# Transposing the gate weights before the output projection's backward pass, and adding the gate biases as one-row matmuls

## The chip, the cores and the metric

The kernel runs on one core of one Trainium2 chip. The metric is device time in microseconds (us); lower is better. Most executions agree within 0.3%. Quoted times are medians. A profile is one execution; its span is some 1.8 us shorter than the measured time (763.3 us against 765.1 us for the profiled execution of the kernel before). Engines: PE (matmul), DVE (VectorE), ACT (ScalarE), POOL (GpSimd), SP (SyncE, which here only issues transfers).

## The reference, cut to what matters

One decode step of a gated attention block, with its backward pass. Outputs are the result and the gradients of nine inputs.

```python
xn = _layernorm(x)
s  = A(xn)    # 32 query heads, 8 KV heads, attention over the last 4096 of 32768 cached rows, then @ wo
g  = silu(B(xn))              # relu(xn @ w1 + b1)**2 @ w2 + b2 : the "gate"
return x + s * g
# reference(): out, and vjp(grad_out) with respect to x, k_cache, v_cache, wq, wo, w1, b1, w2, b2
```

The gradients of the two caches have the caches' full shape, 2 x 8 x 32768 x 128 in bf16. Only the last 4096 rows of each head get a gradient; the other 28672 must be written as zeros. That is 2 x 16 x 28672 x 128 x 2 B = 235 MB of zeros, in 32 parts of 7.34 MB.

## The kernel before

GpSimd queues 31 of the 32 parts of zeros ("zero fills"), from a zeroed tile. They wait only for the load of `wo`, never for arithmetic:

```python
for qi in range(ZQ - 1):                      # ZQ = 32
    ...
        r = zf(*zparts[qi], r, n, rows, rep)  # nc.gpsimd.dma_start(out=v, in_=zeros)
```

The start, cut to the parts that the change touches. Weights and the first V load go into one SP queue; the biases are loaded spread over 128 partitions:

```python
b1_bf = pw.tile([P, FK], BF16, name="b1_bf")       # 128 pieces of 28 B
dma_store.dma_start(out=b1_bf[:], in_=B_b1.rearrange("(p j) -> p j", j=FK))
b2_bf = pw.tile([P, DK], BF16, name="b2_bf")       # 128 pieces of 8 B
dma_store.dma_start(out=b2_bf[:], in_=B_b2.rearrange("(p k) -> p k", k=DK))
dma_load.dma_start(out=w1, ...); dma_load.dma_start(out=w2, ...)   # both in one buffer, tag "k"
wo_in = dma_load.dma_start(out=wo[:], ...); dma_load.dma_start(out=wq[:], ...)
vnat = load(A_v_cache, 0, "v")
... # transposes of x and grad_out; casts b1T<-b1_bf, b2T<-b2_bf; layernorm
... # hps = w1.T @ xn (56 matmuls); hBT = hps + b1T; relu, square; ups = w2.T @ h (56); uT = ups + b2T; silu
... # do_rows, doT_all: backward pass of the output projection (transposes of wo, matmuls)
... # q_rows, qT_all: query projection
for g0 in range(0, len(jobs), 8):                  # 112 transposes of w1 and w2 -> w1T, w2T
    ...
knat = load(A_k_cache, 0, "k")                     # takes over the buffer of w1 and w2
for r in range(NR):                                # 4 rounds of 4 KV heads
    ... # scores of V (dp), scores of K (s), softmax, p_bf, ds_bf
    outer_store(p_bf, bddo, vnat, out_3, r)        # overwrites vnat, stores it
    if r + 1 < NR: vnat = load(A_v_cache, r + 1, "v")
    ...
    outer_store(ds_bf, bdq, knat, out_2, r)
    if r + 1 < NR: knat = load(A_k_cache, r + 1, "k")
```

So the first K load waits for the last gate-weight transpose, and every later load waits for a store. The end:

```python
... # weight gradients; dw2 store; last, in 16 pieces:
        evac(dw1_st[:, k, n0:n0 + n], wps[:, 0:n])
last = nc.sync.dma_start(out=out_6.rearrange("(p k) f -> p k f", k=DK), in_=dw1_st)   # last weight store, 1.8 MB
with tc.issue_after(last.ins):
    fin = nc.sync.dma_start(out=v, in_=zs)                                            # final fill, 7.34 MB
tc.add_manual_dep(fin.ins, sw_fill[-2].ins.name, ...)     # waits for the last-but-one GpSimd fill
```

## Time and profile before

| | before |
|---|---|
| time, median of 3 | 765.2 us (765.09 to 765.24) |
| bytes moved by DMA | 326.73 MB at 428 GB/s |
| end of arithmetic = issue of the last weight store | 724.6 us |
| first K load issued / landed | 95.5 / 123.0 us |

These are lines of the page of the kernel before. The "busy tenths" give the busy share in 40 equal slices of the span, 9 being 90% or more; the queue lines give packets, megabytes and the share of the 16 DMA engines' time:

```profile
PE 387.6 (51%) x4118; PEld 233.5 (31%) x4118; DVE 275.8 (36%) x483; ACT 214.6 (28%) x313; POOL 34.0 (4%) x67
...
DMA  9999999999999999999999999999999999999998
GB/s 382 443 416 422 451 412 425 444 435 416 430 432 450 416 439 429 426 427 446 414 431 435 437 428 427 429 433 440 425 436 437 432 434 422 428 441 425 422 428 379
DMA packets 11833, 326.73 MB, mean 428 GB/s; under 512 B 2898, under 2 KB 2906, under 8 KB 2934
...
q0 software_dynamic: 7360, 227.55, 70.5%
```

The DMA row has no hole: 39 slices of 40 are at 9, and 428 GB/s hold from start to end, while PE is busy 51% of the span. Queue q0 carries the fills, 70% of the bytes. The Trainium skill, "DMA: Bandwidth & Descriptors", section "Specifications", gives 435 GB/s as the ceiling of the fabric; the trace, at 98% of it, agrees.

The windows view shows busy time per engine (with numbers of instructions), the granted PE clock, the DMA share and GB/s in chosen stretches, here near the end of the kernel before:

```profile
core 0: us, PE busy (x) PEld busy (x) DVE busy (x) ACT busy (x) POOL busy (x), PEclk, DMA share, GB/s
...
700.00:720.00 20.00, 18.72 (x43) 5.53 (x42) 13.77 (x22) 12.27 (x21) 0.00 (x0) 0.50 1.04 429
720.00:740.00 20.00, 3.76 (x10) 1.03 (x8) 3.06 (x6) 2.95 (x6) 0.00 (x0) 0.50 0.98 421
740.00:760.00 20.00, 0.00 (x0) 0.00 (x0) 0.00 (x0) 0.00 (x0) 0.00 (x0) 0.50 0.99 424
```

Arithmetic is over soon after 720 us, yet DMA runs at 421 to 424 GB/s until 760 us. These are queued stores and the final fill.

In the timeline of the start, the columns are start, duration, engine, line, operation, tiles; in brackets, how long the engine had been idle and what ended it:

```profile
20.52 0.17 DVE L248 CAST b2T<-b_bf 128x4 f32<-128x4 bf16 x1 [8.93 <-DMA b_bf<-in_B_b_dram]
20.60 0.16 DVE L244 CAST goT<-tp 128x8 f32<-128x8 bf16 x1
...
20.82 1.86 PE L158 MATMUL pp<-xT_f,ones_f 128*128 128x2 f32 x8 [12.72 <-DVE goT L244]
```

On DVE the cast of b2 stands ahead of that of grad_out (`goT`). DVE waits 8.9 us for the landing of b2 (8-byte pieces, issued at 2.0 us), and only after that casts grad_out, whereupon PE starts the layernorm sums, having idled 12.7 us. The transfers that SP issues, in the same columns ("SPq" is SP's queue):

```profile
95.46 0.53 SPq L210 DMA_DIRECT2D nat<-in_A_k_cache_dram  x1
...
507.46 0.54 SPq L210 DMA_DIRECT2D nat<-in_A_k_cache_dram  x1
...
724.57 0.33 SPq L639 DMA_DIRECT2D out_dram<-dw  x1
725.00 0.42 SPq L644 DMA_DIRECT2D out_dram<-zt  x1
```

The chain of waits (start, duration, what) puts long stretches down to K loads. Two of its entries:

```profile
95.46 27.58 DMA nat<-in_A_k_cache_dram
...
507.46 48.59 DMA nat<-in_A_k_cache_dram
```

This chain led back from the last arithmetic. Whether its length is also what the time depends on is the question of this case.

### The profile page before, as it was taken

To read this page: it belongs to the slowest core of one execution; us is meant where nothing else is said; L and a number is where in the kernel's file an instruction comes from. 1 tells how busy PE (TensorE), PEld (TensorE's weight loads), DVE (VectorE), ACT (ScalarE), POOL (GpSimd) and SP (SyncE) were. 2 spreads that over 40 slices of the span, in tenths; PEclk is the share of its full clock that TensorE was granted. 3 is DMA by queue.
4 is the path that set the end of the run, shared out by engine and by line. 5 is a ranking of instruction groups with operands and counts; after the bars stand their busy time and mean duration, and the time that the engine had idled before them with its cause. 6 is when DMAs were issued, how large, how long until landed. Compare 5 with 4: busy or idle time off the path is not lost.

```text
span 763.3 us, 9400 instructions
## 1 busy us (share of the span) xinstructions
PE 387.6 (51%) x4118; PEld 233.5 (31%) x4118; DVE 275.8 (36%) x483; ACT 214.6 (28%) x313; POOL 34.0 (4%) x67
## 2 busy tenths in 40 slices
PE   0666774477003648850576673015073775866800
PEld 0533553333002435420244430014053343423200
DVE  3333342485002347540344653003045152666600
ACT  0144521455000244540112553002013231722500
POOL 0200100010000000000000000000000000000000
PEclk9987997778556886775578587559585675855555
DMA  9999999999999999999999999999999999999998
GB/s 382 443 416 422 451 412 425 444 435 416 430 432 450 416 439 429 426 427 446 414 431 435 437 428 427 429 433 440 425 436 437 432 434 422 428 441 425 422 428 379
DMA packets 11833, 326.73 MB, mean 428 GB/s; under 512 B 2898, under 2 KB 2906, under 8 KB 2934
## 3 DMA queue, kind: packets, MB, share of 16 engines
q0 software_dynamic: 7360, 227.55, 70.5%
q1 hardware_dynamic: 2696, 56.63, 20.9%
q10 hardware_dynamic: 1736, 41.95, 13.2%
q8 instruction: 32, 0.52, 0.3%
q14 instruction: 9, 0.07, 0.0%
HBM read 45.62 MB, written 280.50 MB: 427 GB/s over the span
## 4 chain that ended last, share of the span: by engine, by line
DMA 36%; PE 31%; DVE 12%; ACT 9%; issue 6%; ACTq 0%; DVEq 0%; SPq 0%
DMA nat<-in_A_k_cache_dram 18%; DMA out_dram<-nat 15%; PE ov L421 7%; PE tp L387 4%; ACT nat L150 3%; ACT p_bf L455 2%; DMA b_bf<-in_B_b_dram 2%; PE ps L410 2%; DVE nat L152 2%; ACT tring L150 2%; DVE ds_bf L468 2%; PE s_ps L394 2%; PE wps L588 2%; PE dops L314 2%; PE tp L310 1%
## 5 line engine op out<-in xcount | busy, mean ns | idle before, releaser
L387 PE MATMUL tp<-pperm,nat 128*128 128x128 bf16 x1024 | 91.8, 242 | 180.0 <-DMA nat<-in_A_v_cache_dram 130.0
L152 DVE COPY tring<-tp 128x1024 bf16<-128x1024 bf16 (+1 forms) x98 | 66.1, 689 | 211.0 <-PE tp L387 201.8
L387 PEld LDWEIGHTS <-nat 128*128 128x128 bf16 x1024 | 68.4, 109 | 200.1 <-DMA nat<-in_A_v_cache_dram 131.9
L150 ACT COPY tring<-tp 128x1024 bf16<-128x1024 bf16 (+1 forms) x34 | 34.4, 1011 | 260.2 <-PE tp L387 235.5
L150 ACT CAST nat<-ov 128x512 bf16<-128x512 f32 x160 | 87.4, 590 | 63.6 <-PE ov L421 62.8
L152 DVE CAST nat<-ov 128x512 bf16<-128x512 f32 x96 | 65.5, 690 | 54.3 <-PE ov L421 51.8
L101 POOL DMA_DIRECT2D out_dram<-zt x58 | 32.5, 565 | 529.1 <-DMA out_dram<-zt 507.8
L421 PE MATMUL ov<-bd,ds_bf 128*128 128x512 bf16 x128 | 48.6, 455 | 5.7 <-DVE nat L152 3.7
L421 PE MATMUL ov<-bd,p_bf 128*128 128x512 bf16 x128 | 48.7, 452 | 4.2 <-DVE nat L152 1.4
L410 PE MATMUL ps<-t,nat 128*128 128x16 bf16 x1024 | 28.7, 173 | 14.5 <-issue 7.6
L410 PEld LDWEIGHTS <-nat 128*128 128x128 bf16 x1024 | 28.7, 102 | 17.3 <-issue 12.2
L394 PEld LDWEIGHTS <-zz 128*32 128x32 bf16 x512 | 17.4, 94 | 34.0 <-issue 24.0
L152 DVE CAST wq<-wps 128x512 bf16<-128x512 f32 x16 | 11.0, 690 | 44.2 <-PE wps L581 44.0
L394 PE MATMUL s_ps<-tring,zz 128*32 128x256 bf16 x256 | 19.9, 299 | 12.0 <-ACT tring L150 6.9
L402 PE MATMUL tp<-ident_bf,p_bf 128*128 128x128 bf16 x64 | 7.5, 312 | 34.9 <-ACT p_bf L455 34.9
L150 ACT CAST wq<-wps 128x512 bf16<-128x512 f32 x16 | 9.4, 585 | 53.3 <-PE wps L581 53.3
L455 ACT ACTIVATE p_bf<-e_sb,rl 32x512 bf16<-32x512 f32 x16 | 22.8, 1424 | 3.4 <-DVE rl L452 3.3
L394 PE MATMUL dp_ps<-tring,zz 128*32 128x256 bf16 x256 | 19.4, 305 | 7.7 <-ACT tring L150 4.6
L468 DVE SCALAR_TENSOR_TENSOR ds_bf<-dp_ps,delta,p_bf 32x512 bf16<-32x512 f32 x16 | 21.7, 1359 | 0.2
L421 PEld LDWEIGHTS <-ds_bf 128*128 128x128 bf16 x128 | 12.9, 107 | 20.4 <-issue 17.9
L421 PEld LDWEIGHTS <-p_bf 128*128 128x128 bf16 x128 | 12.8, 109 | 19.8 <-issue 17.1
L402 PEld LDWEIGHTS <-p_bf 128*128 128x128 bf16 x64 | 6.5, 146 | 36.0 <-ACT p_bf L455 36.0
(195 smaller groups left out, 444.4 us busy)
## 6 DMA issues: line engine op xcount, KB each, us to landing
out_dram<-zt POOLq DMA_DIRECT2D x23, 7168.0 KB, 96.7
out_dram<-nat ACTq DMA_DIRECT2D x8, 4096.0 KB, 40.9
out_dram<-zt POOLq DMA_DIRECT2D x7, 3584.0 KB, 71.1
nat<-in_A_v_cache_dram SPq DMA_DIRECT2D x4, 4096.0 KB, 33.8
nat<-in_A_k_cache_dram SPq DMA_DIRECT2D x4, 4096.0 KB, 31.6
out_dram<-zt SPq DMA_DIRECT2D x1, 7168.0 KB, 37.4
out_dram<-zt POOLq DMA_DIRECT2D x2, 3488.0 KB, 64.0
out_dram<-zt POOLq DMA_DIRECT2D x1, 6120.0 KB, 67.4
```

What stands on the lines that cost most here:

```text
L101: sw_fill.append(nc.gpsimd.dma_start(out=v, in_=zs))
L150: nc.scalar.copy(out=out_ap, in_=in_ap)
L152: nc.vector.tensor_copy(out=out_ap, in_=in_ap)
L314: nc.tensor.matmul(dops[0:B, :, :], lhsT=dsT_bf[:, dk, :], rhs=woT[:, :, dk, :], start=(dk == 0), stop=(dk == DK - 1))
L387: nc.tensor.transpose(tp[:, j, :], nat[:, g * CC + half * CH + j, :], pperm[:].rearrange("p b k -> p (b k)"))
L394: nc.tensor.matmul(out_ps[pr * RB:(pr + 1) * RB, half * CH * PB:(half + 1) * CH * PB], lhsT=zbuf[:, pr, o:o + RB], rhs=tT[:, :, pr, :], st ...
L402: nc.tensor.transpose(tp[:, cc, :], src[:, half * CH + cc].rearrange("r k b -> r (k b)"), ident_bf[:, :])
L410: nc.tensor.matmul(ps[:], lhsT=nat[:, g * CC + half * CH + cc, :], rhs=cols[half][:, cc, :, g, :], start=(half == 0 and g == 0 and cc == 0 ...
L421: nc.tensor.matmul(ov[:], lhsT=src[:, cc].rearrange("r k b -> r (k b)"), rhs=bd[:, gh * 4:(gh + 1) * 4, :], start=True, stop=True)
L455: nc.scalar.activation(out=p_bf[rb, :, :, pr], in_=e_sb[rb], func=ACT.Copy, scale=rl[rb, 0:1])
L468: nc.vector.scalar_tensor_tensor(out=ds_bf[rb, :, :, pr], in0=dp_c[rb], scalar=delta[rb, 0:1], in1=p_bf[rb, :, :, pr], op0=ALU.subtract, o ...
L588: nc.tensor.matmul(wps[:], lhsT=o_rows[:, j:N:NJ], rhs=ds_rows[:, :], start=True, stop=True)
```

## The change

Two intentions. The biases come in as single rows and are added inside PSUM by matmuls with one contraction row (`lhsT` = a stretch of the bias row, `rhs` = ones), so that nothing waits for 256 tiny pieces. And the 112 gate-weight transposes stand ahead of the output projection's backward pass, so that the buffer of w1 and w2 is free for the first K load much earlier.

```diff
-        b1_bf = pw.tile([P, FK], BF16, name="b1_bf")
-        dma_store.dma_start(out=b1_bf[:], in_=B_b1.rearrange("(p j) -> p j", j=FK))
+        b1_row = pw.tile([1, F], BF16, name="b1_row")
+        dma_store.dma_start(out=b1_row[:], in_=B_b1.rearrange("(b f) -> b f", b=1))
 ... (b2 in the same way)
+        one_row = pw.tile([1, B], BF16, name="one_row")
+        nc.vector.memset(one_row[:], 1.0)
-        b1T = pw.tile([P, FK], F32, name="b1T")
-        nc.vector.tensor_copy(out=b1T[:], in_=b1_bf[:])
 ... (b2T in the same way)
         for fk in range(FK):
             for k in range(DK):
                 nc.tensor.matmul(hps[:, fk, :], lhsT=w1[:, k, fk:F:FK], rhs=xnT[:, k, :],
-                                 start=(k == 0), stop=(k == DK - 1))
-        nc.vector.tensor_tensor(out=hBT[:], in0=hps[:], in1=b1T[:]..., op=ALU.add)
-        nc.vector.tensor_scalar_max(out=rT[:], in0=hBT[:], scalar1=0.0)
+                                 start=(k == 0), stop=False)
+            nc.tensor.matmul(hps[:, fk, :], lhsT=b1_row[:, fk:F:FK], rhs=one_row[:], start=False, stop=True)
+        nc.vector.tensor_scalar_max(out=rT[:], in0=hps[:], scalar1=0.0)
 ... (ups with b2_row in the same way; the addition of b2T becomes a copy)
-        do_rows = ...   (backward pass of the output projection, doT_all)
-        q_rows = ...    (query projection, qT_all)
         jobs = []       (the 112 transposes of w1 and w2)
 ...
+        do_rows = ...   (moved here, unchanged)
+        q_rows = ...
```

More of the change, by code (lines that the diff above doesn't have):

```diff
@@ L217 @@
         dma_store.dma_start(out=go_bf[:], in_=grad_out.rearrange("b s d -> (b s) d"))
-        b1_bf = pw.tile([P, FK], BF16, name="b1_bf")
-        dma_store.dma_start(out=b1_bf[:], in_=B_b1.rearrange("(p j) -> p j", j=FK))
-        b2_bf = pw.tile([P, DK], BF16, name="b2_bf")
-        dma_store.dma_start(out=b2_bf[:], in_=B_b2.rearrange("(p k) -> p k", k=DK))
+        b1_row = pw.tile([1, F], BF16, name="b1_row")
+        dma_store.dma_start(out=b1_row[:], in_=B_b1.rearrange("(b f) -> b f", b=1))
+        b2_row = pw.tile([1, D], BF16, name="b2_row")
+        dma_store.dma_start(out=b2_row[:], in_=B_b2.rearrange("(b d) -> b d", b=1))
+        one_row = pw.tile([1, B], BF16, name="one_row")
+        nc.vector.memset(one_row[:], 1.0)
         dma_load.dma_start(out=w1, in_=B_w1.rearrange("(p k) f -> p k f", k=DK))
@@ L244 @@
         nc.vector.tensor_copy(out=goT[:], in_=tp[:])
-        b1T = pw.tile([P, FK], F32, name="b1T")
-        nc.vector.tensor_copy(out=b1T[:], in_=b1_bf[:])
-        b2T = pw.tile([P, DK], F32, name="b2T")
-        nc.vector.tensor_copy(out=b2T[:], in_=b2_bf[:])
         meanb = pw.tile([P, B], F32, name="meanb")
@@ L269 @@
                 nc.tensor.matmul(hps[:, fk, :], lhsT=w1[:, k, fk:F:FK], rhs=xnT[:, k, :],
-                                 start=(k == 0), stop=(k == DK - 1))
-        hBT = pw.tile([P, FK, B], F32, name="hBT")
-        nc.vector.tensor_tensor(out=hBT[:], in0=hps[:], in1=b1T[:].unsqueeze(2).to_broadcast([P, FK, B]),
-                                op=ALU.add)
-        nc.vector.tensor_scalar_max(out=rT[:], in0=hBT[:], scalar1=0.0)
+                                 start=(k == 0), stop=False)
+            nc.tensor.matmul(hps[:, fk, :], lhsT=b1_row[:, fk:F:FK], rhs=one_row[:], start=False, stop=True)
+        nc.vector.tensor_scalar_max(out=rT[:], in0=hps[:], scalar1=0.0)
         nc.vector.tensor_tensor(out=h2T_bf[:], in0=rT[:], in1=rT[:], op=ALU.mult)
@@ L279 @@
                 nc.tensor.matmul(ups[:, dk, :], lhsT=w2[:, fk, dk:D:DK], rhs=h2T_bf[:, fk, :],
-                                 start=(fk == 0), stop=(fk == FK - 1))
+                                 start=(fk == 0), stop=False)
+            nc.tensor.matmul(ups[:, dk, :], lhsT=b2_row[:, dk:D:DK], rhs=one_row[:], start=False, stop=True)
         uT = pw.tile([P, DK, B], F32, name="uT")
-        nc.vector.tensor_tensor(out=uT[:], in0=ups[:], in1=b2T[:].unsqueeze(2).to_broadcast([P, DK, B]),
-                                op=ALU.add)
+        nc.vector.tensor_copy(out=uT[:], in_=ups[:])
         enu = pw.tile([P, DK, B], F32, name="enu")
@@ L300 @@
         nc.vector.tensor_copy(out=pk_rows(ds_rows[:]), in_=tp[:])
+        jobs = []
+        for fk in range(FK):
+            for k in range(DK):
+                jobs.append((w1[:, k, fk:F:FK], w1T, fk, k * P))
+        for dk in range(DK):
+            for fk in range(FK):
+                jobs.append((w2[:, fk, dk:D:DK], w2T, dk, fk * P))
+        for g0 in range(0, len(jobs), 8):
+            grp = jobs[g0:g0 + 8]
+            tp = ps_t.tile([P, 8, P], BF16, tag="pt")
+            for j, (src, _, _, _) in enumerate(grp):
+                nc.tensor.transpose(tp[:, j, :], src, ident_bf[:, :])
+            j = 0
+            while j < len(grp):
+                dst, idx, off = grp[j][1], grp[j][2], grp[j][3]
+                n = 1
+                while j + n < len(grp) and grp[j + n][1] is dst and grp[j + n][2] == idx and grp[j + n][3] == off + n * P:
+                    n += 1
+                evac(dst[:, idx, off:off + n * P], tp[:, j:j + n, :].rearrange("p a b -> p (a b)"))
+                j += n
         do_rows = pw.tile([B, N], BF16, tag="rows")
@@ L332 @@
         nc.vector.tensor_copy(out=qT_all[:], in_=tp[:])
-        jobs = []
-        for fk in range(FK):
-            for k in range(DK):
-                jobs.append((w1[:, k, fk:F:FK], w1T, fk, k * P))
-        for dk in range(DK):
-            for fk in range(FK):
-                jobs.append((w2[:, fk, dk:D:DK], w2T, dk, fk * P))
-        for g0 in range(0, len(jobs), 8):
-            grp = jobs[g0:g0 + 8]
-            tp = ps_t.tile([P, 8, P], BF16, tag="pt")
-            for j, (src, _, _, _) in enumerate(grp):
-                nc.tensor.transpose(tp[:, j, :], src, ident_bf[:, :])
-            j = 0
-            while j < len(grp):
-                dst, idx, off = grp[j][1], grp[j][2], grp[j][3]
-                n = 1
-                while j + n < len(grp) and grp[j + n][1] is dst and grp[j + n][2] == idx and grp[j + n][3] == off + n * P:
-                    n += 1
-                evac(dst[:, idx, off:off + n * P], tp[:, j:j + n, :].rearrange("p a b -> p (a b)"))
-                j += n
     kvt = attn.enter_context(tc.tile_pool(name="kvt", bufs=1))
```

## The prediction

> **What bounds the kernel now.** The DMA engines, over the whole span. The page shows 39 of 40 slices at 9 tenths DMA, the last at 8; 326.73 MB moved at a mean of 428 GB/s over 763.3 us. 70.5% of the engines' time is the zero fills (227.55 MB) that GpSimd queues without waiting for any arithmetic. The Trainium skill, "DMA: Bandwidth & Descriptors", section "Specifications", gives 435 GB/s as the fabric ceiling: the trace is at 98% of it, and agrees. PE is 51% busy. The windows view shows DMA below full only in the first 5 us (80, then 291 GB/s) and the last 3 us; the change touches neither.
>
> The chain of waits names compute and loads (K load 18%, PE 31%), but it is not what sets the end: arithmetic ends at 724.5 us, the last GpSimd fill ends at about 728 us, and from there to 762 us only queued stores and the final 7.3 MB fill drain, at 415 to 448 GB/s. A chain that ends earlier only reorders fills and stores.
>
> **What the change does, step by step.**
> 1. The biases become two one-descriptor rows instead of 2 x 128 pieces of 28 and 8 bytes. In the timeline the 8-byte one lands at 20.5 us, and DVE's in-order cast of it holds up goT and the layernorm sums (PE waits 12.7 us). With rows the last input needed is grad_out (7.1 us): the sums should start near 8 us, 12.8 us earlier. Those 256 pieces took 9 ns each on the DMA engines, so the DMA gain is below 1 us.
> 2. Two casts (0.17 us each) and one addition (0.19 us) go. 18 one-row matmuls come in, estimated from the neighbouring matmuls (3.46 us/56 and 2.00 us/56) at 1.0 us. Net: near zero.
> 3. The 112 gate-weight transposes move from mostly 84-96 us to right after the gate (about 23 us), and take about 14 us. They release the buffer that the K load waits for: K is issued near 38-40 us instead of 95.5, behind wq and V in the same queue, and lands near 85-90 us instead of 123.
> 4. dO and q are then ready near 77 and 85 us, like before. Nothing waits for K then; the first softmax comes near 123 us instead of 142.
>
> So the chain of compute moves forward by some 19 us, and arithmetic should end near 705 us instead of 724.5. The Trainium skill's "Key Constraints" (page "Trainium Kernel Development and Optimization") says that DMAs from all queues run on the same 16 engines and interleave; so the earlier K load only displaces fills, which are then still outstanding at the end. Gain on the time: none of the 19 us, perhaps 0.5 us.
>
> **Predicted:** 764.6 us, range 762.0 to 767.5. Faster by over 2%: 1.5%; within 2%: 97%; slower: 1.5%.
>
> **What would show it.** Right: DMA slices as before, same bytes at 427-429 GB/s; K load issued near 40 us; layernorm sums near 8 us; arithmetic ends 10-25 us earlier; the last GpSimd fill ends later than 728 us; a longer pure-DMA tail. Wrong: slices of DMA below 9, or a changed mean rate.
>
> **What would make it wrong.** If DMA starved somewhere (the final fill waits for the last-but-one GpSimd fill; engines might run dry unevenly at the end); if the mix of reads and writes changes the rate; or if the tuned fill pieces balance the 16 engines only for the old order.

## The result, and the profile after

Ratios are the mean time of one kernel's fast runs over that of the other's of the same rounds, so they are not quite the ratio of the medians quoted.

| | before | after |
|---|---|---|
| time, median of 6 | 765.17 us (765.05 to 765.32) | 765.33 us (765.05 to 765.44) |
| ratio, 95% interval | | 1.0001 (0.9988 to 1.0014) |
| layernorm sums start | 20.8 us | 10.6 us |
| first K load issued / landed | 95.5 / 123.0 us | 39.0 / 87.2 us |
| first softmax (exponential) | 142.2 us | 123.1 us |
| last softmax | 574.7 us | 541.9 us |
| end of arithmetic = last weight store issued | 724.6 us | 687.3 us |
| last large piece of a GpSimd fill ends | 727.2 us | 746.4 us |

The rows below the ratio are read from one profiled execution of each kernel. In it the arithmetic ends 37.2 us earlier, and the time is the same. The page of the changed kernel shows the same bytes at the same rate:

```profile
DMA  9999999999999999999999999999999999999998
GB/s 382 433 417 442 413 444 418 443 421 431 439 422 441 419 443 427 425 430 430 442 418 441 427 433 433 421 436 433 433 438 436 417 442 423 426 441 427 431 437 363
DMA packets 11549, 326.73 MB, mean 428 GB/s; under 512 B 2612, under 2 KB 2621, under 8 KB 2650
...
q0 software_dynamic: 7360, 227.55, 70.3%
```

Only 284 tiny packets are gone (11833 to 11549), net: the bias pieces and their completion writes. The windows at the end of the changed kernel:

```profile
700.00:720.00 20.00, 0.00 (x0) 0.00 (x0) 0.00 (x0) 0.00 (x0) 0.00 (x0) 0.50 1.03 439
720.00:740.00 20.00, 0.00 (x0) 0.00 (x0) 0.00 (x0) 0.00 (x0) 0.00 (x0) 0.50 1.08 425
740.00:760.00 20.00, 0.00 (x0) 0.00 (x0) 0.00 (x0) 0.00 (x0) 0.00 (x0) 0.50 1.02 422
```

From 700 us on no engine computes, and DMA still moves 422 to 439 GB/s (the last column): the pure transfer tail, to the end of the span, has grown from 39 us to 76 us. In the timeline of the start:

```profile
10.33 0.17 DVE L246 CAST goT<-tp 128x8 f32<-128x8 bf16 x1 [2.40 <-PE tp L245]
...
10.55 1.86 PE L158 MATMUL pp<-xT_f,ones_f 128*128 128x2 f32 x8 [0.26 <-DVE goT L246]
...
24.03 0.21 PE L269 MATMUL hps<-one_row,b_row 1*128 1x2 bf16 x1
...
24.18 0.40 PE L267 MATMUL hps<-xnT,w_129 128*128 128x2 bf16 x4
...
24.51 0.21 PE L269 MATMUL hps<-one_row,b_row 1*128 1x2 bf16 x1
```

`goT` waits for no bias any more. The one-row matmuls (L269) show a cost that will matter below. The transfers that SP issues:

```profile
38.99 0.53 SPq L210 DMA_DIRECT2D nat<-in_A_k_cache_dram  x1
...
500.32 0.54 SPq L210 DMA_DIRECT2D nat<-in_A_k_cache_dram  x1
...
687.33 0.33 SPq L635 DMA_DIRECT2D out_dram<-dw  x1
726.06 0.39 SPq L640 DMA_DIRECT2D out_dram<-zt  x1
```

And of the waits of SP's queue (who waited for whom: total, times, longest), the largest new one is this:

```profile
SPq L640 <- DMA out_dram<-zt: 38.3, 1, 38.3
```

The final fill now stands ready from 687.7 us, but waits 38.3 us for the last-but-one GpSimd fill. This could be the place into which the gain went, so it is tested.

### The profile page after: what moved, and what is told of

Its sections match the earlier page's. It is cut to its first block, busy times and chain, and to the rows that moved or that the text cites. A ratio compares the mean times of both kernels' runs of the same rounds, so it can differ in the third digit from the quotient of the medians.

```text
span 763.6 us, 9426 instructions
## 1 busy us (share of the span) xinstructions
PE 387.7 (51%) x4127; PEld 236.2 (31%) x4136; DVE 274.5 (36%) x481; ACT 216.7 (28%) x314; POOL 34.2 (4%) x67
## 2 busy tenths in 40 slices
DMA packets 11549, 326.73 MB, mean 428 GB/s; under 512 B 2612, under 2 KB 2621, under 8 KB 2650
## 3 DMA queue, kind: packets, MB, share of 16 engines
HBM read 45.62 MB, written 280.50 MB: 427 GB/s over the span
## 4 chain that ended last, share of the span: by engine, by line
PE 33%; DMA 28%; DVE 12%; ACT 10%; issue 7%; ACTq 0%; DVEq 0%; SPq 0%
DMA out_dram<-nat 14%; DMA nat<-in_A_v_cache_dram 8%; PE tp L383 7%; PE ov L417 6%; DMA nat<-in_A_k_cache_dram 5%; ACT tring L150 3%; ACT p_bf L451 2%; DVE tring L152 2%; ACT nat L150 2%; PE s_ps L390 2%; DVE ds_bf L464 2%; PE wps L584 2%; PE ps L406 1%; PE dp_ps L390 1%; DVE nat L152 1%
## 5 line engine op out<-in xcount | busy, mean ns | idle before, releaser
L383 PE MATMUL tp<-pperm,nat 128*128 128x128 bf16 x1024 | 87.9, 235 | 150.6 <-DMA nat<-in_A_v_cache_dram 132.7
L383 PEld LDWEIGHTS <-nat 128*128 128x128 bf16 x1024 | 64.8, 105 | 169.6 <-DMA nat<-in_A_v_cache_dram 134.6
L101 POOL DMA_DIRECT2D out_dram<-zt x58 | 32.6, 566 | 529.2 <-DMA out_dram<-zt 508.1
L417 PE MATMUL ov<-bd,p_bf 128*128 128x512 bf16 x123 | 46.7, 448 | 5.4 <-DVE nat L152 1.4
L406 PEld LDWEIGHTS <-nat 128*128 128x128 bf16 x1024 | 28.6, 102 | 20.7 <-issue 15.5
```

Source lines behind the costliest of these rows:

```text
L101: sw_fill.append(nc.gpsimd.dma_start(out=v, in_=zs))
L383: nc.tensor.transpose(tp[:, j, :], nat[:, g * CC + half * CH + j, :], pperm[:].rearrange("p b k -> p (b k)"))
L406: nc.tensor.matmul(ps[:], lhsT=nat[:, g * CC + half * CH + cc, :], rhs=cols[half][:, cc, :, g, :], start=(half == 0 and g == 0 and cc == 0 ...
L417: nc.tensor.matmul(ov[:], lhsT=src[:, cc].rearrange("r k b -> r (k b)"), rhs=bd[:, gh * 4:(gh + 1) * 4, :], start=True, stop=True)
```

## The experiments

Three theories were on trial.

- **Main theory.** DMA is full from start to end. The bytes set the time as long as the arithmetic ends early enough for its last stores; the change makes the arithmetic end earlier, which only gives slack.
- **Rival 1.** Only bytes matter; the arithmetic is far from the limit in both kernels, so its end is of no consequence at all.
- **Rival 2.** The chain of arithmetic sets the time, and the gain is lost in a new wait (the final fill's) or in the transfer rate.

Twelve kernels ran. Times with an interval had 3 rounds; the others are a single run, whose state is then unknown; each such figure below is of one execution. The kernel before, run beside each group, gave 765.3 to 765.6 us. All results were correct, except that kernels with fills taken away leave those rows unwritten.

### 1. Two fills less, in both kernels

```diff
         for qi in range(ZQ - 1):
+            if qi in (27, 28):
+                continue
             r = 0
```

> The kernel before without two of its whole zero fills (14.7 MB of the 326.7 MB; a wrong result on purpose in those rows). Main theory (the DMA engines are full, and before the change the arithmetic ends only just early enough): 14.7 MB are worth 34 us, but the arithmetic still ends near 724 us and the last weight store and the final fill (9.2 MB, 21.5 us at 428 GB/s) are only issued then, so the time falls by only about 18 us, to 745 to 750 us. Rival 1 (the order of arithmetic never matters, only bytes): it falls by the full 34 us to 731 us. Rival 2 (the chain of waits is what sets the end): it falls by less than 5 us.

> The changed kernel without the same two zero fills (wrong result on purpose). Main theory: its arithmetic ends near 687 us, so the bytes alone set the end and the full 34 us are saved: 729 to 733 us, 14 to 18 us faster than the kernel before without the two fills. Rival 1 (only bytes matter in both): 731 us, the same as the kernel before without them. Rival 2 (a loss at the tail or in the rate cancels the earlier arithmetic): no faster than the kernel before without the two fills, near 748 us.

Measured: the kernel before without the two fills 750.65 us (749.67 to 751.64), ratio to the kernel before 0.9807 (0.9793 to 0.9822). The changed kernel without them 731.35 us, ratio 0.9553 (0.9534 to 0.9572); one of its four runs (743.28 us) counts as slow by its length and is left out of the ratio. Its granted clock, 0.685, is hardly below that of the others (0.689 to 0.702), and it was not profiled, so its cause is open. The 750.65 us lie just above the 745 to 750 us that the main theory gave, the 731.35 us inside its range. So the same removal of bytes saves 15 us in one kernel and 34 us in the other. The windows view shows why. First the kernel before without the two fills, then the changed one:

```profile
690.00:700.00 10.00, 6.51 (x24) 4.55 (x25) 4.80 (x11) 0.58 (x1) 0.00 (x0) 0.50 0.16 67
700.00:710.00 10.00, 10.00 (x24) 3.29 (x23) 7.46 (x12) 6.43 (x11) 0.00 (x0) 0.50 0.00 0
```

```profile
690.00:700.00 10.00, 0.00 (x0) 0.00 (x0) 0.00 (x0) 0.00 (x0) 0.00 (x0) 0.50 0.96 411
700.00:710.00 10.00, 0.00 (x0) 0.00 (x0) 0.00 (x0) 0.00 (x0) 0.00 (x0) 0.50 0.98 423
```

In the first, DMA runs dry (67 GB/s, then 0) while PE still computes the stores' data; its last weight store is issued at 724.6 us, exactly as with all fills. In the second the arithmetic has ended by then and DMA stays full. This is against rival 1 (the two kernels differ by 19 us once bytes are fewer) and against rival 2 (the earlier end of the arithmetic is worth its time as soon as the bytes let it through).

The time here ends 25.6 us after the profiled issue of the last weight store (profiled run 750.26 us, issue 724.64 us): that store and the final fill, 9.2 MB, must still go out, which at 428 GB/s is 21.4 us. (1.8 us of the rest is the difference between the span and the measured time.) This gives a formula to test: **time = the larger of what the bytes take and (issue of the last weight store + 25.6 us).** For the kernel before the second term is 750.2 us: 15 us of slack. For the changed kernel, in its profiled execution, it is 712.9 us: 52 us.

### 2. Dead work in the last round

```diff
+            for _ in range(75):
+                nc.vector.memset(s_rows[:], 0.0)
             nc.vector.tensor_copy(out=s_rows[:], in_=sps[:])
```

> The kernel before with some 75 dead memsets on VectorE in the last round, which hold the arithmetic back by about 40 us (their real length is read from the trace). Main theory: there is next to no slack, so with the arithmetic ending near 764 us the last weight store and final fill (21.5 us) follow it: 783 to 790 us. Rival 1 (only bytes matter): 765 us. Rival 2 (chain of waits): 805 us.

> The changed kernel with the same dead memsets. Main theory: it has some 37 us more slack than the kernel before; with the arithmetic ending near 727 us the time stays at 764 to 769 us. Rival 1: 765 us. Rival 2 (chain of waits): 805 us.

Measured: 765.18 us and 765.09 us. The experiment missed its aim. The 75 memsets (0.485 us each) were slotted in between other DVE work, and in the kernel before the last weight store came at 732.7 us, only 8 us later. In the changed kernel it came at 728.8 us, but most of this shift is not the memsets'. Their first one starts at 583.7 us, and the execution had fallen behind long before: the second K load was issued at 215.1 instead of 204.8 us, the last one at 508.1 instead of 500.3 us, and that one landed at 556.3 instead of 524.0 us, after late completion writes (experiment 5). So its last softmax came at 575.2 us. In the five other profiles with the changed kernel's code up to there (the changed kernel itself, experiments 1, 3 and 4; experiment 1 lacks two late fills) it came at 541.9 to 544.6 us; in the four of the kernel before, at 574.6 to 575.0 us. The earlier end of the arithmetic is thus no fixed property of the changed kernel: in one execution of six its lead was gone before the memsets began, and with them 11 us of slack were left. Both runs agree with the formula (758.3 and 754.4 us, below what the bytes take), but they don't tell the theories apart. "Next to no slack" was also wrong: 8 us of delay cost the kernel before nothing.

### 3. Dead work at the very end

The delay was moved to where nothing can fill it: between two evictions of the last piece of the last weight gradient.

```diff
             evac(dw1_st[:, k, n0:n0 + n], wps[:, 0:n])
+            if k == DK - 1 and n0 + n == F:
+                for _ in range(200):        # 400 in the third kernel
+                    nc.vector.memset(dw1_st[:, k, n0:n0 + n].bitcast(F32), 0.0)
+                evac(dw1_st[:, k, n0:n0 + n], wps[:, 0:n], eng="dve")
```

> The kernel before with 200 small dead memsets on VectorE between two evictions of the very last chunk of the last weight gradient: the end of arithmetic moves one to one, by some 35 to 60 us (read from the trace), and nothing else can fill the wait in. The two-fill run put the end some 25.5 us after the issue of the last weight store (750.3 us against 724.6 us). Main theory: time = the larger of 765 us and that issue + 25.5 us; so with, say, 40 us of memsets, 790 us. Rival 1 (only bytes matter): 765 us.

> The changed kernel with the same 200 memsets. Main theory: the same formula with the issue at 687.3 us + the memsets; with 40 us of memsets (727 us) it stays at 765 us; up to about 52 us of delay cost nothing, where the kernel before bears only about 15. Rival 2 (the earlier end of arithmetic is already used up, e.g. by the wait for the last-but-one fill): it is slower by the length of the memsets, as the kernel before.

> The changed kernel with 400 memsets, twice the delay. Main theory: the same formula, 687.3 us + the delay + 25.5 us; with 80 us, 793 us, so that half of it shows. Rival 1 (only bytes matter, slack without limit): 765 us.

Measured: the kernel before with 200 memsets 802.88 us; the changed kernel with 200 memsets 765.62 us, with 400 memsets 816.01 us. What SP issues in the first of these:

```profile
777.28 0.33 SPq L643 DMA_DIRECT2D out_dram<-dw  x1
777.71 0.39 SPq L648 DMA_DIRECT2D out_dram<-zt  x1
```

The last weight store went from 724.6 to 777.3 us, so the memsets took 52.7 us, and the time grew by 37.3 us: 15 us of them were free. In the changed kernel they took 51.5 us (store at 738.9 us) and cost nothing (765.62 against 765.33 us). Twice as many moved the store to 790.4 us, and the formula's 816.0 us was measured. Rival 1 falls, and rival 2 too: one and the same delay costs 37 us in one kernel and nothing in the other.

### 4. The final fill without its wait

```diff
-    tc.add_manual_dep(fin.ins, sw_fill[-2].ins.name, ...)
```

The zeroed tile is only read, and the rows of the final fill are written by nothing else, so that no data hazard hangs on this wait.

> The changed kernel without the wait of the final fill for the last-but-one GpSimd fill (38.3 us on SyncE in the trace of the changed kernel; no data hazard hangs on it). Main theory: the final fill is issued near 688 us instead of 726 us and the other fills land later by as much; same bytes, same time, within 0.3% of 765 us. Rival 2 (the gain went into this new wait): faster, down to about 740 us.

Measured: 765.17 us, ratio 0.9995 (0.9978 to 1.0012). The final fill was issued at 689.1 us instead of 726.1 us. The 38.3 us wait was the largest new entry in SP's table of waits, and taking it away gives nothing: same bytes, same time.

### 5. Each half of the change alone

> The kernel before with only the gate-weight transposes moved ahead of the output projection's backward pass. Main theory: 765 us within 0.3%. In the trace the layernorm sums stay near 20.8 us (they wait for the bias casts), the K load is issued near 48 to 52 us instead of 95.5, and the first softmax comes near 132 to 136 us (142 before, 123 with both parts): the bias wait still delays dO and q by some 10 us. If the bias rows were of no use to the chain, the first softmax would come near 123 us.

> The kernel before with only the bias rows and one-row matmuls. Main theory: 765 us within 0.3%; layernorm sums near 8 us, the K load issued near 83 us (12.8 us earlier), and the first softmax some 10 us earlier than before, near 130 us. If the order alone made the gain, it would stay at 142 us.

The diffs are the respective part of the change. Measured: the order alone 765.81 us, the biases alone 787.01 us.

| | before | order alone | biases alone | both |
|---|---|---|---|---|
| layernorm sums start | 20.8 | 21.4 | 8.4 | 10.6 |
| first K load issued | 95.5 | 45.5 | 85.3 | 39.0 |
| first softmax | 142.2 | 129.5 | 140.5 | 123.1 |
| last K load issued | 507.5 | 508.0 | 554.0 | 500.3 |
| last softmax | 574.7 | 576.3 | 614.8 | 541.9 |
| last weight store issued | 724.6 | 726.7 | 761.4 | 687.3 |
| that + 25.6 us | 750.2 | 752.3 | 787.0 | 712.9 |
| measured time | 765.2 | 765.8 | 787.0 | 765.3 |

(All in us.) The biases alone were 22 us slower in their one run, which no theory had expected. Nor did either half meet its forecast at the start. With the order alone, K was issued at 45.5 us (48 to 52 expected) and the first softmax came at 129.5 us (132 to 136 expected). With the biases alone the sums began 12.4 us earlier, but the first softmax came at 140.5 us and not near 130: K, issued 10 us earlier, landed at 120.8 us, only 2 us earlier. The formula holds to 0.1 us: the last weight store came late,

```profile
761.39 0.33 SPq L635 DMA_DIRECT2D out_dram<-dw  x1
```

and before it DMA ran dry, as the DMA row of this run's page shows:

```profile
DMA  9999999999999999999999999999999999999099
```

The time follows. So the question becomes why its chain ran late although it started 12 us earlier. The table shows that a lead at the start doesn't survive: the order alone is 12.7 us ahead at the first softmax and 1.6 us behind at the last. The DMA records show where leads are won and lost. A transfer ends with a 4-byte completion write on each of its DMA engines. Usually it takes under 0.1 us, but many took 2.2, 4.3, 6.4, 8.5, 10.6, 12.7 or 14.8 us. These are near multiples of 2.1 us, and one 57,344-byte piece of a fill took 2.15 us. Single ones of 3.2, 7.4 and 15.4 us fit less well. This table was tabulated from those records (a record ends some 0.5 us before the semaphore that tells of the landing):

| kernel | late completion writes seen at the loads and stores of the rounds |
|---|---|
| before | last K load: 15 engines done by 528.2 us, the last data of the sixteenth at 538.7 us, its completion write from 540.8 us took 14.8 us: landed at 556.1 us. Earlier, the first V load: all 16, of 8.5 to 10.6 us; the second V and K loads: one of 12.7 us each |
| after | last K load: all 16 completed by 523.7 us, none took over 0.1 us: landed at 524.0 us. Earlier: third K load 7.4 us, two of a first-round store, 6.4 us each |
| order alone | last K load: one of 12.7 us and one of 14.8 us: landed at 557.4 us |
| after, memsets in the last round (experiment 2) | second V load: two of 10.6 us; second K load: one of 15.4 us; last K load: four of 6.4 to 14.8 us: landed at 556.3 us |
| biases alone | first V load: all 16, of 8.5 to 9.0 us; first K load: 11 writes of 8.5 to 14.8 us; third K load: 12.7 us; third V-gradient store: 10 writes of 10.6 to 12.7 us; last V load: 4.3 to 10.6 us; last K load: 2.2 to 8.5 us |
| 29 fills taken away (next experiment) | none of 2 us or more that began after 70 us, in either kernel (the last piece of the two fills left to GpSimd ends at 77 and 80 us); earlier, at the first V load, 8.5 to 10.8 us in the kernel before and 2.2 us in the changed one |

The reading that fits is that a completion write can stand behind up to seven fill pieces that its engine has already taken up. The Trainium skill, "DMA: Bandwidth & Descriptors", section "Queues, rings and completion order", says that the completion increment "lands only after every earlier write from that SDMA engine, across its queues". The steps of 2.1 us, and the absence of late writes once the fills are over, agree. No run isolates it further (other piece sizes were not tried). What decides which loads meet late writes is open: the kernel before met them at its last K load in all four profiles (landed at 556.1 to 556.4 us), the changed kernel in one of six, and the biases-alone kernel, with the most, was run once.

### 6. Hardly any fills

```diff
         for qi in range(ZQ - 1):
+            if qi < 29:
+                continue
             r = 0
```

> The kernel before with 29 of the 32 zero fills taken away (213 MB; wrong result on purpose), so that bytes no longer bound it and the chain of loads, arithmetic and stores sets the time: 530 to 600 us.

> The changed kernel with the same 29 fills taken away. Main theory: here the earlier start shows in full, but it is only the start: 8 to 20 us faster than the kernel before without these fills (K then loads in about 10 us, so most of what the transposes' order gives is gone and the 12 us of the biases remain). Rival 2 (the new order costs as much as it gives somewhere later in the arithmetic): no difference, within 3 us.

Measured: 581.26 us before, 573.70 us after. The DMA rows of the two pages, first the kernel before, show that DMA is idle for much of the time:

```profile
DMA  8999912400068840008973001797100024660598
```

```profile
DMA  8999980000578700067870005787000051660699
```

With the bytes out of the way the change is worth 7.6 us, a little below the 8 to 20 us expected. The first softmax came 11.4 us earlier (119.8 against 131.2 us) and the last one 11.1 us earlier (418.2 against 429.3 us). So the lead of the start survives the rounds when there is no fill to wait behind; 3.5 us of it are lost in the last stretch (why was not looked into). In the kernel before, the first K load now takes 13.6 us (issued at 97.0, landed at 110.6 us) instead of 27.6 us, so an early issue has less to win. How the 11.4 us divide between order and biases was not tested without fills.

### All runs against the formula

| kernel | last weight store issued + 25.6 us | what the bytes take | measured |
|---|---|---|---|
| before | 750.2 | 765.3 | 765.2 |
| after | 712.9 | 765.3 | 765.3 |
| before, two fills less | 750.2 | 731 | 750.3 (profiled run) |
| after, two fills less | 712.4 | 731 | 731.4 |
| before, dead work late | 802.9 | 765.3 | 802.9 |
| after, dead work late | 764.5 | 765.3 | 765.6 |
| after, twice the dead work | 816.0 | 765.3 | 816.0 |
| biases alone | 787.0 | 765.3 | 787.0 |
| before, 29 fills less | 581.2 | not needed | 581.3 |
| after, 29 fills less | 573.7 | not needed | 573.7 |

The 765.3 us are the measured time of the two full kernels (326.73 MB at 428 GB/s are 763.4 us, and 1.8 us lie outside the span), and the 25.6 us come from the run of the kernel before with two fills less, so those three rows are no test of the formula; the other seven are. The 731 us are worked out as 765.3 us less 14.68 MB at 428 GB/s. No experiment pointed to a version with all its fills that would be faster than both kernels: 326.73 MB have to move, and they already move at 428 GB/s.

## Why the prediction was right, point by point

- **The time: right, for the stated reason.** 764.6 us were predicted and 765.33 us measured. The bytes (326.73 MB) and the rate (428 GB/s) are unchanged. Experiments 1 and 3 show that the end of the arithmetic had 15 us of slack before, and 52 us in the profiled execution of the changed kernel; experiment 2 shows an execution where most of these 52 us had been lost again, at no cost.
- **Where the earlier arithmetic goes: right.** As predicted, it moves fills to the end (last large piece of a fill at 746.4 instead of 727.2 us) and makes a longer tail of pure DMA. Experiment 4 shows that the new wait of the final fill costs nothing.
- **First K load and first softmax: right.** 38 to 40 us was predicted for the issue, 39.0 us measured; 85 to 90 us for the landing, 87.2 us measured; 123 us for the first softmax, 123.1 us measured. The steps on the way agree too: dO was ready at 76.5 us and q at 85.5 us (77 and 85 predicted), and the chain to the first softmax no longer holds a wait for K.
- **"The sums should start near 8 us": right for the biases, not in this order.** With the biases alone they start at 8.4 us. With both parts, the first 16 gate-weight transposes stand ahead of grad_out's transposes on PE (8.1 to 10.1 us), and the sums start at 10.6 us.
- **"18 one-row matmuls ... at 1.0 us": too small.** The stage of `hps` took 6.7 us (19.9 to 26.6 us) instead of 3.5 us. In the lines above, one group of four matmuls plus its one-row matmul takes 0.48 us (24.03 to 24.51 us), against 3.46 us / 14 = 0.25 us without: 0.23 us for each one-row matmul, not the 0.06 us of its neighbours. (With the biases alone, where no transposes are mixed in, a group takes 0.48 us too.) In the second stage, `ups`, a group of 14 with its one-row matmul takes 0.68 us instead of 2.00 us / 4 = 0.50 us: 0.18 us each. All 18 cost some 3.9 us; the time, bound by bytes, shows nothing of it. The Trainium skill, "TensorEngine Tiling (Array Packing)", section "Key Properties", says that changing the tiling mode drains TensorE; whether a one-row matmul does that is not shown here.
- **"Right after the gate (about 23 us)": wrong in place, right in effect.** The transposes don't follow the gate but fill the waits of the layernorm and the gate from 8.1 us on. The gate's gradient (`dsT_bf`) came at 33.4 us, only 2.5 us earlier than before.
- **"Arithmetic should end near 705 us": too little; 687.3 us.** The predicted 19 us were there at the first softmax (142.2 to 123.1 us). But the forecast carried them unchanged to the end. In the trace the lead had shrunk to 7.1 us at the issue of the last K load (507.5 to 500.3 us), and was 32 us at its landing, because the kernel before met a late engine and a late completion write there (556.1 us) and the changed kernel didn't (524.0 us). Some 4 us more came in the last stretch (32.8 us at the last softmax, 37.2 us at the end). So the figure of 37 us is in part luck of the profiled execution: in experiment 2 the changed kernel's code met the late writes at the last K load, and its last softmax came at 575.2 us, as in the kernel before. Experiment 5 also shows how loose this is: starting earlier, the biases alone ended 37 us later in their one run.

## What to carry to other kernels

Where the DMA row is full from the first slice to the last, ask of a change to the arithmetic only whether the last stores still get out in time: time = the larger of (bytes / rate) and (issue of the last store + the transfers that must follow it). An earlier end of the arithmetic is then slack. It can be measured by a delay that nothing can fill in, or by taking bytes away. And a lead at the start of a chain whose loads and stores share engines with a deep queue of large pieces doesn't carry to its end unchanged: look at the landings, not only at the issues.

## What the Trainium skill lacked or had wrong

- "DMA: Bandwidth & Descriptors" states the order rule for completion writes, but gives no size for it: its fixed cost of a DMA is about 2 us. Here, behind a deep queue of 57,344-byte fill pieces (2.15 us each), completion writes took up to 15.4 us, nearly all in steps of 2.1 us; with 29 of the 32 fills gone, none that began after 70 us took 2 us or more.
- The same page, in "Where 436 GB/s comes from", says that for transfers between HBM and SBUF the HBM side, some 358 GB/s per core, binds. Taken alone this is wrong here: with one core running this program, it held 428 GB/s for 763 us. The page itself has the missing condition elsewhere (its 425 GB/s at 16 MB is for one core alone, some 358 GB/s for each of two cores that stream). Its measured table is of loads; 86% of the bytes were writes to HBM (280.50 of 326.1 MB).
- No page that was read gives the cost of a one-row accumulating matmul between full ones: 0.23 us each here between groups of 4 and 0.18 us between groups of 14, against 0.06 and 0.04 us for the 128-row matmuls around it.
